# Gated mix of sliding-window attention and a GELU layer: one exponential tile per block of 128 keys, a masking step for both halves at once, wider steps of the division, and part-wise tiles in the last stage

## The chip, the cores and the metric

The kernel runs on one core of a Trainium2 chip. The metric is device time in microseconds (us), from the start to the end of one execution; the figure compared is the median of several executions.

## The reference

One input x of 2048 rows and 512 columns goes through two branches, and a gate per row mixes them:

```python
g = sigmoid((x * gate_w).sum(-1, keepdims=True))
a = attention(x)            # 32 heads of 16, window of 256 keys, causal; then @ wo
b = gelu(x @ w1 + b1) @ w2 + b2     # 512 -> 1792 -> 512
out = g * a + (1 - g) * b
```

In the attention, query i sees key j where 0 <= i - j < 256. The softmax is over these keys, and its result is multiplied with the values.

## The kernel before, in words

**Numbers.** All dense products (q, k, v, w1, w2, wo) are made in three matmuls each (`mm3`, L100): an operand is split into a rounded high part and the low remainder, and high*high, high*low and low*high are summed in PSUM. So each weight and each activation tile needs a copy on ScalarE (the high part) and a subtraction on VectorE or GpSimd (the low part).

**How the order is set.** The kernel is scheduled by hand: every engine runs its instructions in the order in which the program records them, and all DMAs stand in the one queue of SyncE (SP). While it records, the program keeps a clock of its own, `now`. `tick(ns)` moves it on with each group of matmuls, `after(ns, fn)` puts a step down for later, and `need(key)` runs such steps ahead until the one that makes `key` is recorded. The constants (`DIVS`, `HOLD`, `LAND0`, `LANDO`, `NORM`) are these delays: they say behind which other instructions a step stands, not when it runs. An instruction whose input isn't there holds up everything behind it on its engine.

**Stages.** `dense()` yields the dense matmuls in order: q, k and v of the four tiles of 512 rows (`qkv`, t = 0 to 3), the two layers of the GELU branch in eight turns (`mlp`, half of the 1792 features for one tile each), and the last product with wo (`final(t)`, t = 0 to 3). The attention runs between these matmuls (the loop at L859): for each of 8 groups of 4 heads and each of 16 blocks of 128 keys, one step `u` records four score matmuls for the row maxima (`att_max`, 12 blocks ahead), four for the exponentials (`att_exp`), and dense matmuls that fill the step.

**Maxima.** VectorE reduces the scores `sm` to maxima (`jm`, `M`, L472); `att_rows` turns them round (`nm`, `tt`), and GpSimd copies them as extra rows into `qs` (L495), so that the next score matmul `st` subtracts them.

**Exponentials.** `att_exp` (L501) works on a block of 128 keys in two halves `hf` of 64 keys, and in two pairs `pr`. ScalarE writes exp(st) into a tile `pt` (L531), one tile per half, 14 buffers. When both pairs of a half are written, `sel` clears the corners outside the window: four `affine_select` on GpSimd (L525; two partition halves, two edges) of 64 partitions by 2 x 64 numbers, or, in the last 12 blocks, one minimum on VectorE with a mask of 0 and 3e38 (L520).

**Values.** After every fourth block, `att_pvs` multiplies 6 blocks of `pt` with the values in `vbuf` (L553) and sums numerators and the denominator in two PSUM tiles, `pv_st` and `pv_sm`. The first pair of matmuls reads the first block and the second half of the last block. `vbuf` has two slots; `att_load_v` loads one (L453). ScalarE and VectorE add the two PSUM tiles into `nd` (L574, L577), which goes to DRAM (`ND`).

**Division.** For a pair of groups, `att_norm(t, c)` loads the denominators `den` from DRAM, takes the reciprocal (L595), stores them as `RD` (L598), loads the numerators `num` and the reciprocals spread over 16 rows `rb` (L603), multiplies them on VectorE (L607) and stores the result as `OT` (L610). `DIVS` holds the delays of these five steps.

**Last stage.** `load_o(t)` loads the four parts of `OT` of a tile (`ot`, L640) and splits them (L643, L646). `final(t)` makes 4 blocks of 12 matmuls each into PSUM tiles of which there are two; ScalarE scales the GELU branch (`ao`, L790), VectorE adds g times the PSUM tile (L817), and the sum is stored (L822). The GELU results come back through `load_y` (`qd<-YB`, `kd<-YB`, L784).

**Start.** In the first tile, `gate(0)` multiplies rows of x with the gate weights `gwb` on VectorE (`xj`, L269), and `load_xr(1)` loads the rows of the next tile into the buffers that this frees.

Of the kernel before, what the change touches and what calls it, by code (L numbers as in the profile page):

```python
# [32 lines left out]
def gated_mix(ctx: ExitStack, tc: tile.TileContext, x, wqkv, wo, w1, b1, w2, b2, gate_w, out):  # L33
# [94 lines left out]

    wk4 = wqkv.rearrange("(c p) f -> p c f", p=128)
    wt, raws = {}, {}  # L130

    def load_raw(key, early=False):
# [10 lines left out]
        elif early or now[0] < RAWS:  # L143
            raw = sb.tile([128, 2, 320], F32, tag="pt", bufs=PTS, name=f"raw_{kind}{i}")
            raw = raw.rearrange("p a b -> p (a b)")[:, 0:T]
        else:
            raw = sb.tile([128, T], F32, tag="raw", bufs=2, name=f"raw_{kind}{i}")
# [185 lines left out]
    def qkv(t):  # L333
# [17 lines left out]
        for n, (kind, j) in enumerate(pieces):  # L351
# [150 lines left out]
    def att_exp(g_, kb, i):  # L502
# [4 lines left out]
        if pr == 0:  # L507
            pts[g_, kb, hf] = sb.tile([128, 2, 320], F32, tag="pt", bufs=PTS, name=f"pt{g_}_{kb}_{hf}")
        pt = pts[g_, kb, hf]
# [5 lines left out]

        def sel():
            n = 1 + (w == W + 64)
            if g_ * NKB + kb >= NU - LEAD:
                v = pt.rearrange("p a (e x) -> p a e x", x=64)[:, :, 0:4 * n - 3:4]
                nc.vector.tensor_tensor(v, v, cut[:, 0:n].unsqueeze(1).broadcast_to([128, 2, n, 64]), op=ALU.min)  # L520
            else:
                for r in (0, 64):
                    for e in range(n):
                        v = pt[r:r + 64, :, W * e:W * e + 64]
                        nc.gpsimd.affine_select(out=v, in_=v, pattern=[[0, 2], [1 - 2 * e, 64]],  # L525
                                                compare_op=ALU.is_ge, fill=0.0, base=-e,
                                                channel_multiplier=2 * e - 1)
            done.add(("pt", g_, kb, hf))

        def exp():  # L530
            nc.scalar.activation(pt[:, pr, :w], p[:, :w], AF.Exp, scale=SCALE)  # L531
            if pr == 1:
                after(500, sel)
# [3 lines left out]
    def att_pvs(u):  # L537
# [21 lines left out]
        for j, pair in enumerate(pairs):  # L559
# [3 lines left out]
            for i in range(4):  # L563
                for hf, b in enumerate(pair):
                    k0 = b * 128 + hf * 64
                    q, e = max(k0, c * T), min(k0 + W + 64, S, (c + 1) * T)
                    mm(b, i, hf, q, e, lambda r: pts[g_, b, hf][r:r + 64, i // 2, q - k0:e - k0],
# [61 lines left out]
    def load_o(t, cs=range(NC)):  # L629

        if ("o", t) not in xts:
            if t % 2 == 0:
                v = sb.tile([128, NC, 2, T], F32R, tag="xt", bufs=1, name=f"ot{t}")
                xts["o", t] = [v[:, c] for c in range(NC)]
            else:
                xts["o", t] = [sb.tile([128, 2, T], F32R, tag="h", bufs=7, name=f"ot{t}_{c}") for c in range(NC)]
        ot = xts["o", t]
        for c in cs:
            need(("o", t, c))
# [306 lines left out]
```

## Time and profile before

| | us |
|---|---|
| median of 3 runs | 779.35 (777.29 to 779.69) |
| the profiled execution | 778.52 |
| its span in the profile | 776.8 |
| TensorE (PE) busy | 744.8 (96%) |
| VectorE (DVE) busy | 515.9 (66%) |
| ScalarE (ACT) busy | 431.6 (56%) |
| GpSimd (POOL) busy | 424.6 (55%) |

The span is what the profile's rows add up to; 1.7 us of the execution lie around it. A row of the timeline gives start, duration, engine, line, operation, output and inputs with shapes, and in brackets how long the engine had been idle and what ended that. SPq is the queue of SyncE, in which a row is the issue of a DMA and not its transfer; in the chain of waits, a row "DMA x<-y" is the time from issue to landing. PEclk is the clock granted to TensorE as a part of full speed. Matmuls overlap: the next one starts some 0.23 us after a 512-column one, though each is shown as 0.39 us long, and a busy PE may still not run at its peak.

### The profile page before, as it was taken

Reading aid. Unit: us, or ns where it says so; the run is one execution under the profiler, and the core shown is the slowest. Engines: PE = TensorE matmul, PEld = TensorE weight load, DVE = VectorE, ACT = ScalarE, POOL = GpSimd, SP = SyncE. Lnnn points to the kernel's source line nnn. Section 1 sums busy time; section 2 is a strip of 40 time slices with the busy share of each in tenths; the row PEclk is TensorE's granted clock in tenths of the full one; section 3 lists DMA queues with packets and bytes.
Section 4 is the critical chain, followed back from the end, with each engine's and each line's share of the span. In section 5 each row is a group of like instructions: output and inputs, shape, how many; then the busy total and the mean of one; then the engine's idle time right before and its main releaser. Section 6 shows DMA issues by size and latency. Waiting matters only on the chain.

```text
span 776.8 us, 18309 instructions
## 1 busy us (share of the span) xinstructions
PE 744.8 (96%) x6104; PEld 615.8 (79%) x6104; DVE 515.9 (66%) x1572; ACT 431.6 (56%) x973; POOL 424.6 (55%) x1174
## 2 busy tenths in 40 slices
PE   8999999989999999999999998999999999998798
PEld 6888888768788888888887877888888888876677
DVE  3532325789658877976896789568768866963443
ACT  4434523359448745854884587358647844974431
POOL 3200000239867976996797679669867976800000
PEclk9999999999999999999999999999999999999999
DMA  9979899998895798799676899986999998437672
GB/s 272 357 234 401 262 375 279 238 309 193 242 258 120 169 253 204 169 218 257 153 169 166 214 235 226 259 178 134 205 222 245 206 262 198 113 101 222 203 237 106
DMA packets 179262, 172.14 MB, mean 222 GB/s; under 512 B 56672, under 2 KB 122976, under 8 KB 179168
## 3 DMA queue, kind: packets, MB, share of 16 engines
q1 hardware_dynamic: 179168, 170.97, 83.4%
q8 instruction: 48, 0.79, 0.5%
q14 instruction: 46, 0.38, 0.2%
HBM read 108.53 MB, written 62.39 MB: 220 GB/s over the span
## 4 chain that ended last, share of the span: by engine, by line
PE 65%; DMA 13%; POOL 6%; DVE 6%; issue 3%; SPq 3%; ACT 3%; DVEq 0%; ACTq 0%; POOLq 0%
PE sm L467 7%; PE st L513 6%; PE pv_sm L553 6%; POOL pt L525 5%; DMA rb<-RD 5%; PE y L101 5%; PE u L101 4%; PE y L103 4%; PE y L102 4%; PE u L103 4%; PE u L102 4%; PE qk L101 4%; PE qk L103 3%; PE qk L102 3%; PE v L101 2%
## 5 line engine op out<-in xcount | busy, mean ns | idle before, releaser
L525 POOL TENSOR_SCALAR_AFFINE_SELECT pt<-pt 64x128 f32<-64x128 f32 x872 | 294.1, 357 | 102.7 <-ACT pt L531 82.0
L472 DVE CUSTOM_DVE_ANT_0 jm<-sm,mask 128x320 bf16<-128x320 f32 (+4 forms) x512 | 238.0, 465 | 74.4 <-PE sm L467 46.6
L531 ACT ACTIVATE pt<-st 128x320 f32<-128x320 f32 (+4 forms) x512 | 206.5, 423 | 132.3 <-PE st L513 128.5
L467 PE MATMUL sm<-kd,qd 96*128 96x320 f32 (+4 forms) x512 | 157.7, 311 | 5.2 <-DVE M L472 3.7
L513 PE MATMUL st<-qs,ks 128*128 128x320 f32 (+4 forms) x512 | 155.1, 307 | 2.4 <-ACT pt L531 2.4
L495 POOL CAST qs<-tt 4x256 fp32r<-4x256 f32 x256 | 116.9, 457 | 39.1 <-DVE tt L488 15.6
L467 PEld LDWEIGHTS sm<-kd,qd 96*128 96x128 f32 x512 | 96.5, 188 | 30.5 <-DVE M L472 9.1
L513 PEld LDWEIGHTS st<-qs,ks 128*128 128x128 f32 x512 | 98.0, 191 | 22.9 <-ACT pt L531 3.9
L101 PE MATMUL y<-w,h 128*128 128x512 f32 x224 | 90.7, 405 | 0.0
L103 PE MATMUL y<-w,h 128*128 128x512 f32 x224 | 88.6, 395 | 0.0
L553 PE MATMUL pv_st<-pt,vbuf 64*32 64x320 f32 (+4 forms) x1408 | 76.8, 355 | 12.2 <-POOL pt L525 4.4
L102 PE MATMUL y<-w,h 128*128 128x512 f32 x224 | 87.7, 392 | 0.0
L553 PE MATMUL pv_sm<-pt,vbuf 64*32 64x320 f32 (+4 forms) x1408 | 78.7, 355 | 2.4 <-DVE M L472 1.2
L101 PE MATMUL u<-mx,w 128*128 128x512 f32 x196 | 80.2, 409 | 0.0
L103 PE MATMUL u<-mx,w 128*128 128x512 f32 x196 | 77.5, 395 | 0.0
L102 PE MATMUL u<-mx,w 128*128 128x512 f32 x196 | 76.8, 392 | 0.0
L553 PEld LDWEIGHTS pv_sm<-pt,vbuf 64*32 64x32 f32 x1408 | 56.3, 108 | 19.9 <-DVE M L472 3.1
L553 PEld LDWEIGHTS pv_st<-pt,vbuf 64*32 64x32 f32 x1408 | 50.5, 108 | 13.4 <-POOL pt L525 7.3
L288 DVE TENSOR_TENSOR qke<-qk,qke 128x512 fp32r<-128x512 f32 x32 | 22.1, 690 | 48.1 <-ACT qke L285 40.0
L307 POOL MEMSET vx<- 128x32 f32 x16 | 2.5, 155 | 93.0 <-DMA kd<-SK 23.8
L574 ACT ACTIVATE nd<-pv_st 128x512 f32<-128x512 f32 x32 | 19.1, 597 | 57.5 <-PE pv_sm L553 53.4
L103 PEld LDWEIGHTS y<-w,h 128*128 128x128 f32 x224 | 42.1, 188 | 10.0
(142 smaller groups left out, 1336.3 us busy)
## 6 DMA issues: line engine op xcount, KB each, us to landing
kd<-SK SPq DMA_DIRECT2D x32, 384.0 KB
qs<-SQ SPq DMA_DIRECT2D x64, 192.0 KB
mx<-XT SPq DMA_DIRECT2D x24, 512.0 KB
SQ<-qke SPq DMA_DIRECT2D x16, 512.0 KB
SK<-qke SPq DMA_DIRECT2D x16, 512.0 KB
ND<-nd SPq DMA_DIRECT2D x32, 256.0 KB
raw_w<-in_B_w_dram SPq DMA_DIRECT2D x28, 256.0 KB
ks<-SK SPq DMA_DIRECT2D x32, 192.0 KB
```

The lines of the kernel that those rows point to most:

```text
L101: nc.tensor.matmul(p, lh, rh, start=first, stop=False)
L102: nc.tensor.matmul(p, lh, rl, start=False, stop=False)
L103: nc.tensor.matmul(p, ll, rh, start=False, stop=last)
L288: nc.vector.tensor_sub(e[:, 1 - h], p, f32(e[:, h]))
L467: nc.tensor.matmul(p[:, :w], qd[0:96, n, pr, 128 * j:128 * (j + 1)], kd[0:96, n, pr, k1 - w:k1], start=True, stop=True)
L472: nc.vector.tensor_tensor_reduce(junk[:, :w], p[:, :w], mask[:, 320 - w:320], 1.0, -3e38, ALU.add, ALU.max, M[:, 2 * (b % RB) + hb, pr:pr ...
L495: nc.gpsimd.tensor_copy(dst, src.unsqueeze(1).broadcast_to([4, 2, RB, 32]))
L513: nc.tensor.matmul(p[:, :w], ks[:, slot(g_, kb // NB), pr, at:at + 128], qs[:, pr, k0:k0 + w], start=True, stop=True)
L525: nc.gpsimd.affine_select(out=v, in_=v, pattern=[[0, 2], [1 - 2 * e, 64]], compare_op=ALU.is_ge, fill=0.0, base=-e, channel_multiplier=2 * ...
L531: nc.scalar.activation(pt[:, pr, :w], p[:, :w], AF.Exp, scale=SCALE)
L553: nc.tensor.matmul(pv[r // 64][32 * i:32 * i + 32, q - c * T:e - c * T], vts[g_, b // NB][r:r + 64, v:v + 32], rhs(r), start=start, stop=s ...
L574: nc.scalar.activation(nd, pv[0], AF.Copy)
```

## The change

Six things change. (1) A tile `pt` now holds a whole block of 128 keys (both halves), with 7 buffers for 14, and raw weights and output rows take half of such a tile each (`half_pt`). (2) Where GpSimd masks, it does so for both halves in one set of four `affine_select` of 64 x 4 x 64, behind the fourth exponential; the last of every four blocks keeps a set for each half. (3) The gate of the first tile and the load behind it are put 4 us later. (4) `vbuf` is asked for one step earlier. (5) In the division, the multiplication and the store stand further behind the loads; the last group pair uses the short delays for all four tiles, and its four sums are stored at once. (6) In the last stage each part of `ot` is a tile of its own, in buffers of the weights (t = 2) or of `h` (t = 1, 3), asked for only when its `OT` is stored, and tile t + 2 is asked for in the middle of `final(t)`.

```diff
+    spare = []
+    def half_pt(name):
+        if not spare:
+            v = sb.tile([128, 2, 2, 320], F32, tag="pt", bufs=PTS, name=name)
+            v = v.rearrange("p h a b -> p h (a b)")
+            spare.extend(v[:, h, 0:T] for h in (1, 0))
+        return spare.pop()
...
                 if n == 1:
-                    gate(0)
-                    load_xr(1)
+                    after(4000, gate, 0)
+                    after(4000, load_xr, 1)
...
+        n = 1 + (w == W + 64)
+        late = g_ * NKB + kb >= NU - LEAD
+        both = not late and kb % NB < NB - 1
         def sel():
...
+                hs = slice(0, 2) if both else slice(hf, hf + 1)
                 for r in (0, 64):
                     for e in range(n):
-                        v = pt[r:r + 64, :, W * e:W * e + 64]
-                        nc.gpsimd.affine_select(out=v, in_=v, pattern=[[0, 2], [1 - 2 * e, 64]],
+                        v = pt[r:r + 64, hs].rearrange("p h a c -> p (h a) c")[:, :, W * e:W * e + 64]
+                        nc.gpsimd.affine_select(out=v, in_=v, pattern=[[0, v.shape[1]], [1 - 2 * e, 64]],
...
-            if pr == 1:
+            if pr == 1 and (hf == 1 or not both):
                 after(500, sel)
...
-            after(HOLD if g_ * NT + c < NQ - 2 else 800, store)
+            after(HOLD if g_ * NT + c < NQ - 4 else 800, store)
...
-                after(NORM if g_ * NT + c < NQ - 2 else 3500, att_norm, c, g_ // 2)
+                after(NORM if g_ * NT + c < NQ - 4 else 3500, att_norm, c, g_ // 2)
...
-            done.add(("o", t, c))
-        for ns, fn in zip(DIVS[c == NC - 1 and t >= NT - 2], (rcp, keep, back, mul, store)):
+            after(REACH, done.add, ("o", t, c))
+        for ns, fn in zip(DIVS[c == NC - 1], (rcp, keep, back, mul, store)):
...
+    def load_part(t, c, land, skew):
+        ot = xts["o", t]
+        if ("o", t, c) not in done:
+            return after(500, load_part, t, c, LANDO, 0)
+        if t:
+            tag, bufs = ("w", 14) if t == 2 else ("h", 7)
+            ot[c] = sb.tile([128, 2, T], F32R, tag=tag, bufs=bufs, name=f"ot{t}_{c}")
+        nc.sync.dma_start(f32(ot[c][:, 1]), OT[t][c])
...
     def final(t):
+        if t == 0:
+            load_o(1)
...
-            if t == NT - 2 and b == 2:
-                load_o(t + 1, range(NC - 1, NC))
+            if b == 2 and t < 2:
+                load_o(t + 2, range(NC - t))
+            if b == 1 and t == 2:
+                load_o(NT - 1, range(NC - 1, NC))
...
-        if u % NB == 1 and u >= 0:
+        if u % NB == 0 and u >= 0:
             att_load_v(*divmod(u // NB, NT))
...
-PTS = 14
+PTS = 7
+REACH = 2500.0
-DIVS = ((6000, 9000, 12000, 18500, 22000), (4500, 5700, 8500, 13500, 15000))
+DIVS = ((6000, 9000, 12000, 21500, 23500), (4500, 5700, 8500, 17000, 18500))
```

The order of the matmuls on PE stays as it was. Three places on other engines follow. First SyncE's queue early in the attention, at the second load of `vbuf` (SV1 are the values of the second tile; SK2 keys, XT3 the kept x, ND0_0 the first sums). Before:

```order
L425 DMA ks_181<-SK2_76 48x2x64
L730 DMA XT3_85<-xt3_984 128x1024 x4
L622 DMA mx00_2152<-XT0_82 128x1024
L447 DMA qs_180<-SQ3_73 48x2x512 x2
L453 DMA vbuf_175<-SV1_79 128x8x34
L581 DMA ND0_0_90<-nd0_0_2114 128x512
```

After:

```order
L435 DMA ks_181<-SK2_76 48x2x64
L463 DMA vbuf_175<-SV1_79 128x8x34
L750 DMA XT3_85<-xt3_980 128x1024 x4
L636 DMA mx00_2123<-XT0_82 128x1024
L457 DMA qs_180<-SQ3_73 48x2x512 x2
L595 DMA ND0_0_90<-nd0_0_2084 128x512
```

The load of `vbuf` now stands ahead of the four XT stores, the mx load and both qs loads.

Second, VectorE near the end, at the first division of the last group pair (pt7_10 and pt7_11 are blocks 10 and 11 of the last group, num0_3 the product for tile 0, yo the GELU result). Before:

```order
L520 TENSOR_TENSOR pt7_10_1_10715<-pt7_10_1_10715,cut_151 128x2x2x64
L520 TENSOR_TENSOR pt7_11_0_10731<-pt7_11_0_10731,cut_151 128x2x2x64
L748 SCALAR_TENSOR_TENSOR yo_10722<-y3_11_10679,ya3_11_10092 128x512
L607 TENSOR_TENSOR num0_3_10738<-num0_3_10738,rb0_3_10740 128x512
L595 RECIPROCAL den1_3_10752<-den1_3_10752 128x32
L520 TENSOR_TENSOR pt7_11_1_10749<-pt7_11_1_10749,cut_151 128x2x2x64
```

After:

```order
L533 TENSOR_TENSOR pt7_10_10243<-pt7_10_10243,cut_151 128x2x2x64
L621 TENSOR_TENSOR num0_3_10193<-num0_3_10193,rb0_3_10195 128x512
L533 TENSOR_TENSOR pt7_11_10271<-pt7_11_10271,cut_151 128x2x2x64
L768 SCALAR_TENSOR_TENSOR yo_10262<-y3_11_10222,ya3_11_9644 128x512
L609 RECIPROCAL den1_3_10248<-den1_3_10248 128x32
L533 TENSOR_TENSOR pt7_11_10271<-pt7_11_10271,cut_151 128x2x2x64
```

The product num0_3 stands two instructions further ahead; the reciprocal of den1_3 keeps its place in front of the second mask of block 11.

Third, SyncE's queue at the same time (ks are keys of the last tile, qd<-YB0 and YB1 GELU results). Before:

```order
L591 DMA den0_3_10570<-ND0_3_93 128x1x32
L428 DMA ks_181<-SK3_77 48x8x128
L423 DMA ks_181<-SK3_77 48x7x128
L425 DMA ks_181<-SK3_77 48x2x64
L581 DMA ND1_3_97<-nd7_1_10651 128x512
L598 DMA RD0_3_109<-den0_3_10570 128x32
L453 DMA vbuf_175<-SV2_80 128x8x34
L784 DMA qd_182<-YB0_126 128x2x512 x2
L603 DMA num0_3_10738<-ND0_3_93 128x1x512
L603 DMA rb0_3_10740<-RD0_3_109 128x1x512
```

After:

```order
L605 DMA den0_3_10052<-ND0_3_93 128x1x32
L612 DMA RD0_3_109<-den0_3_10052 128x32
L617 DMA num0_3_10193<-ND0_3_93 128x1x512
L617 DMA rb0_3_10195<-RD0_3_109 128x1x512
L595 DMA ND1_3_97<-nd7_1_10189 128x512
L438 DMA ks_181<-SK3_77 48x8x128
L433 DMA ks_181<-SK3_77 48x7x128
L435 DMA ks_181<-SK3_77 48x2x64
L463 DMA vbuf_175<-SV2_80 128x8x34
L804 DMA qd_182<-YB0_126 128x2x512 x2
```

The loads num0_3 and rb0_3 now stand ahead of the keys, of vbuf and of YB0. For the next tile it is the other way round: the store of RD1_3, which stood ahead of the two loads of YB1, now stands behind them.

More of the change, by code (lines that the diff above doesn't have):

```diff
@@ L143, in load_raw @@
         elif early or now[0] < RAWS:
-            raw = sb.tile([128, 2, 320], F32, tag="pt", bufs=PTS, name=f"raw_{kind}{i}")
-            raw = raw.rearrange("p a b -> p (a b)")[:, 0:T]
+            raw = half_pt(f"raw_{kind}{i}")
         else:
+            spare.clear()
             raw = sb.tile([128, T], F32, tag="raw", bufs=2, name=f"raw_{kind}{i}")
@@ L635, in load_o, with hi, lo @@
             else:
-                xts["o", t] = [sb.tile([128, 2, T], F32R, tag="h", bufs=7, name=f"ot{t}_{c}") for c in range(NC)]
+                xts["o", t] = {}
+        for n, c in enumerate(cs):
+            load_part(t, c, LAND0 if t == 0 else LANDO, 700 * n)
+    def load_part(t, c, land, skew):
         ot = xts["o", t]
-        for c in cs:
-            need(("o", t, c))
-            nc.sync.dma_start(f32(ot[c][:, 1]), OT[t][c])
-            def hi(c=c):
-                nc.scalar.activation(ot[c][:, 0], f32(ot[c][:, 1]), AF.Copy)
-            def lo(c=c):
-                nc.vector.tensor_sub(ot[c][:, 1], f32(ot[c][:, 1]), f32(ot[c][:, 0]))
-                done.add(("ot", t, c))
-            n = cs.index(c)
-            land = LAND0 if t == 0 else LANDO
-            after(land + 700 * n, hi), after(land + 700 * n + 600, lo)
+        if ("o", t, c) not in done:
[4 more added lines that the diff above has]
+        nc.sync.dma_start(f32(ot[c][:, 1]), OT[t][c])
+        def hi():
+            nc.scalar.activation(ot[c][:, 0], f32(ot[c][:, 1]), AF.Copy)
+        def lo():
+            nc.vector.tensor_sub(ot[c][:, 1], f32(ot[c][:, 1]), f32(ot[c][:, 0]))
+            done.add(("ot", t, c))
+        after(land + skew, hi), after(land + skew + 600, lo)
     TURNS = [(0, 3), (0, 0), (0, 1), (0, 2), (1, 2), (1, 0), (1, 1), (1, 3)]
@@ L793, in final @@
     def final(t):
+        if t == 0:
+            load_o(1)
         ot = xts["o", t]
-        if t < NT - 1:
-            load_o(t + 1, range(NC) if t < NT - 2 else range(NC - 1))
         for b in range(NB):
```

21 lines of the change are left out of this document (9 added, 12 removed).

## The prediction

> **What bounds the kernel now.** I read the page first: TensorE is busy nearly all the time.
>
> ```profile
> span 776.8 us, 18309 instructions
> PE 744.8 (96%) x6104; PEld 615.8 (79%) x6104; DVE 515.9 (66%) x1572; ACT 431.6 (56%) x973; POOL 424.6 (55%) x1174
> ```
>
> So 32.0 us of the span have no matmul, and the change leaves the matmuls as they are: its gain lies in those 32.0 us and in a slower clock, nowhere else. Next the view of busy time by stage. Its columns are the stretch, its length, then PE, PEld, DVE, ACT and POOL busy, the granted clock, DMA share and GB/s.
>
> ```profile
> 250.00:450.00 200.00, 196.11 (x1931) 164.20 (x1929) 154.62 (x510) 124.23 (x282) 159.71 (x446) 1.00 0.84 197
> 700.00:720.00 20.00, 16.28 (x156) 12.86 (x154) 6.25 (x14) 8.31 (x23) 0.00 (x0) 0.91 0.82 229
> 720.00:740.00 20.00, 15.59 (x147) 12.57 (x148) 9.77 (x19) 7.69 (x13) 0.00 (x0) 0.94 0.52 180
> ```
>
> In the attention PE idles 2%; from 700 to 740 us it idles 3.7 + 4.4 = 8.1 us of 40, and the clock falls to 0.91 and 0.94 there. The last stage is where most is lost. Then the timeline of PE, for the idle time before a matmul and what ended it:
>
> ```profile
> 18.66 0.50 PE L101 MATMUL qk<-ks,qk 128*128 128x512 f32 x1 [0.96 <-DVE qke L288]
> 205.69 0.25 PE L553 MATMUL pv_st<-pt,vbuf 64*32 64x64 f32 x2 [1.94 <-DMA vbuf<-SV]
> 341.31 0.30 PE L553 MATMUL pv_sm<-pt,vbuf 64*32 64x64 f32 x2 [1.03 <-DVE M L472]
> 483.69 0.30 PE L553 MATMUL pv_st<-pt,vbuf 64*32 64x64 f32 x4 [1.69 <-POOL pt L525]
> 706.17 0.25 PE L553 MATMUL pv_st<-pt,vbuf 64*32 64x64 f32 x2 [3.55 <-issue]
> 722.15 0.25 PE L553 MATMUL pv_st<-pt,vbuf 64*32 64x64 f32 x2 [2.32 <-DVE pt L520]
> 737.90 0.76 PE L101 MATMUL a<-wo,ot 128*128 128x512 f32 x1 [2.26 <-DVE ao L817]
> 751.42 0.47 PE L101 MATMUL a<-wo,ot 128*128 128x512 f32 x1 [0.83 <-DVE ao L817]
> ```
>
> The row at 483.69 stands for nine like it, which the view of waits sums (us in total, times, longest):
>
> ```profile
> PE pv_st L553 <- POOL pt L525: 4.4, 5, 1.7
> PE pv_sm L553 <- POOL pt L525: 1.1, 4, 0.3
> ```
>
> Five causes: 0.96 us at the start, 1.94 for vbuf, 5.5 for GpSimd's masks, 1.03 at 341 us and 3.55 + 2.32 + 2.26 + 0.83 = 8.96 near the end, 18.4 of the 32.0 us. The timeline of VectorE says what is behind three of them.
>
> ```profile
> 16.96 1.03 DVE L269 CUSTOM_DVE_ANT_0 xj<-xr,gwb 128x512 bf16<-128x512 f32 x1 [3.47 <-DMA gwb<-in_gate_w_dram]
> 340.06 0.79 DVE L607 TENSOR_TENSOR num<-num,rb 128x512 f32<-128x512 f32 x1 [1.33 <-DMA rb<-RD]
> 704.84 0.69 DVE L607 TENSOR_TENSOR num<-num,rb 128x512 f32<-128x512 f32 x1 [4.41 <-DMA rb<-RD]
> 705.71 0.69 DVE L520 TENSOR_TENSOR pt<-pt,cut 128x256 f32<-128x256 f32 x2
> ...
> 749.32 0.69 DVE L607 TENSOR_TENSOR num<-num,rb 128x512 f32<-128x512 f32 x1 [2.71 <-DMA rb<-RD]
> ```
>
> And the view of waits has all of this kind:
>
> ```profile
> DVE num L607 <- DMA rb<-RD: 20.1, 8, 5.0
> ```
>
> VectorE stands at the product num and waits for rb, four of the eight times from 704 to 750 us. Behind it in its order stand the masks of the last blocks (705.71) and the evictions of the last stage, and PE waits for those: each of the four late stalls of PE starts in a wait of num. The "issue" at 706.17 is this too, since the masks are done at 706.4.
>
> **The change part by part.** *Gate of the first tile.* The gate product waits 3.47 us for gwb, and the eviction qke behind it comes late. 4 us later in the order, qke of two more matmul groups stands ahead, and gwb has landed. The loads of xr move behind one store of keys and the first of XT; their first transpose comes over 7 us later, which hides them. Gain 0.9, between 0 and the 0.96 of the row.
>
> *vbuf.* From the queue of SyncE and the chain of waits:
>
> ```profile
> 187.87 3.66 SPq L730 DMA_DIRECT2D XT<-xt  x4
> 199.86 0.54 SPq L453 DMA_DIRECT2D vbuf<-SV  x1
> 199.86 5.69 DMA vbuf<-SV
> ```
>
> vbuf now stands ahead of XT, so is issued at about 188 and lands at 188 + 5.7 = 194, 11 us ahead of need. Its slot is free, as it is the first use. Later vbuf loads wait for the value matmuls just recorded, and the store of nd waits behind them; none was late before. Gain 1.9 (0 to 1.94).
>
> *Masks.* The groups of GpSimd, shapes apart (count, busy us, mean ns):
>
> ```profile
> L525 POOL TENSOR_SCALAR_AFFINE_SELECT pt<-pt 64x128 f32<-64x128 f32 x872 | 294.1, 357 | 102.7 <-ACT pt L531 82.0
> L80 POOL TENSOR_SCALAR_AFFINE_SELECT cut<-cut 64x64 f32<-64x64 f32 x4 | 0.9, 236 | 0.1
> masks.py:199 POOL TENSOR_SCALAR_AFFINE_SELECT ident<-ident 128x128 f32<-128x128 f32 x1 | 0.3, 292 | 0.1
> ```
>
> Seven groups have 14 blocks of 8 selects and 2 of 4, the eighth 4 blocks of 8: 7 x 120 + 32 = 872. Three blocks of every four now take half as many, of 256 numbers: 11 blocks of 4 and one of 2 a group, 3 of 4 in the eighth, 7 x 46 + 12 = 334. The fourth blocks keep 7 x 28 + 8 = 204 of 128. No row has 256 numbers. From 64 to 128 a select grows by 292 - 236 = 56 ns undisturbed (0.88 ns a number) or 357 - 236 = 121 ns as it runs in the attention (1.9 ns). So 128 more cost 113 to 242 ns: 470 to 599 ns; the upper bound is twice 357, with nothing saved. I take 470, as the attention's 357 holds waiting beside the work. GpSimd then saves 668 x 0.357 - 334 x 0.47 = 238.5 - 157.0 = 81.5 us of its 424.6 (38.4 at 599).
>
> By the Trainium skill's "GPSIMD Engine Reference", section 3.1, an element costs about 2.6 cycles in a two-input add; at that and its 1.2 GHz, 128 more would be an estimated 277 ns, a select 634, and the saving 27 us. By that rule a third of the stall would go (1.8 us), and the sum would be 2.7 us smaller; the 0.88 ns between the two set-up rows speak against it.
>
> PE waits because GpSimd is behind, not because one mask is slow: ahead of 483.69 it ran 28 selects back to back.
>
> ```profile
> 475.24 10.77 POOL L525 TENSOR_SCALAR_AFFINE_SELECT pt<-pt 64x128 f32<-64x128 f32 x28
> ```
>
> The last block of every four, for which PE waits, keeps its two short sets; ahead of it stand three blocks at half the count, some 12 x (2 x 0.357 - 0.47) = 2.9 us less backlog, against stalls of 1.69 us at most. That later masks of the first half wait for the fourth exponential costs nothing: the values need them blocks later. Gain 4.5, between 1.8 and 5.5.
>
> *Division in the attention.* num stands some three maxima later in the order.
>
> ```profile
> L472 DVE CUSTOM_DVE_ANT_0 jm<-sm,mask 128x320 bf16<-128x320 f32 x448 | 217.7, 486 | 69.1 <-PE sm L467 44.4 <-PE st L513 3.6 <-DVE M L472 0.5
> ```
>
> rb landed 1.33 us late, three maxima take 1.46, so the 1.03 us at 341 go; the other such waits cost PE little. Gain 1.0 (0 to 1.03).
>
> *Last group.* The chain of waits shows how long the DMAs of a division take:
>
> ```profile
> 432.42 6.01 DMA RD<-den
> 577.65 3.30 DMA RD<-den
> 581.00 4.65 DMA rb<-RD
> 695.78 8.96 DMA rb<-RD
> 705.55 3.04 DMA OT<-num
> ```
>
> For tile 0 rb was issued at 695.78, behind two loads of YB0, and took 8.96 us. VectorE before that:
>
> ```profile
> 686.32 0.69 DVE L670 SCALAR_TENSOR_TENSOR x1h<-sqh,x1h 128x512 f32<-128x512 f32 x1 [1.27 <-ACT sqh L667]
> ...
> 697.72 0.43 DVE L520 TENSOR_TENSOR pt<-pt,cut 128x256 f32<-128x256 f32 x1 [0.47 <-ACT pt L531]
> ```
>
> The reciprocal now stands just ahead of the first of these two rows, so RD goes out by about 687; rb follows 3.3 to 6.0 us later, ahead of YB0, and lands 4.7 to 9.0 us after: between 695 and 702. num, behind the mask of the last row, is reached at about 698. The stall of 3.55 us then shrinks to between 0 and 3. For tile 1, RD1_3 now stands behind YB1, and SyncE waits for its landing before rb; but everything starts 3.5 us earlier, and num stands three masks later. For tiles 2 and 3 num stands behind one more eviction or more, and rb is issued a few us earlier against its eviction. Each of the four can be cured or be half left: gain 6.5 of 8.96, between 2 and 8.96. Who is late next: the masks themselves, 0.3 to 0.4 us each.
>
> *Clock.* At 0.91 and 0.94, 16.28 and 15.59 us of matmuls lose 1.5 + 0.9 = 2.4 us; the dips stand beside the idle time. If most of that goes, about half: 1.2 (0 to 2.4).
>
> *Tiles of the last stage.* t = 2 no longer waits for the one xt tile. No matmul waited long for that, so 0; it costs where loads come later, which is the second rival.
>
> *Given back.* PE comes earlier to the maxima of a busy VectorE:
>
> ```profile
> PEld sm L467 <- DVE M L472: 9.1, 17, 1.3
> ```
>
> Mean 0.54 us; I count four more such waits, 2.0 us (0 to 4).
>
> **Sum**: 0.9 + 1.9 + 4.5 + 1.0 + 6.5 + 1.2 - 2.0 = 14.0 us. The profiled execution took 778.52, 1.7 over its span and 0.8 under the median of 779.35. 778.5 - 14.0 = 764.5, and 765 as a median. All best ends: 778.5 - 20.8 = 758 (the 18.4 us of stalls and 2.4 of clock); all worst: 1.8 + 2 - 4, or 779.
>
> **The rivals.** *The last stage keeps its stalls.* DMAs there are slow because the queues are full (share 0.82 from 700 to 720 us), not because of their order: rb stays late, num blocks again, RD1_3 behind YB1 does it. Then the tail and clock terms go: 0.9 + 1.9 + 4.5 + 1.0 - 2.0 = 6.3, giving 772 to 773. For it speaks that 1 MB of YB is loaded either way, against it that rb of tile 0 overtakes it. Chance 0.17.
>
> *Slower: the last stage's loads come late.* Each ot is asked for only after its OT is recorded as stored, and stands behind output stores which wait for evictions. The split of a part that has landed is two passes over 128x512; at the 0.69 of VectorE's rows an estimated 1.4 us. From RD to the split it is 3.30 + 4.65 + 3.04 + 1.4 = 12.4 us at best, by the rows above, and 6.01 + 8.96 + 3.04 + 1.4 = 19.4 at worst; a tile of `final` gives 48 matmuls at
>
> ```profile
> 751.89 0.23 PE a L102
> ```
>
> 11.0 us. Where the chain of a tile starts only as the tile before it starts, 1.4 to 8.4 us are uncovered. It decides from 6.3 us on, which is what the other parts bring. At 6 us for two tiles: 778.5 - 6.3 + 12 = 784. Against it: in the order the OT store of tile 2 stands in front of tile 1's first output, and tile 3's in front of tile 1's last, a whole tile ahead. Chance 0.08.
>
> *Nothing moves.* The masks grow to 714 ns and PE, freed at one engine, waits for the next (VectorE is busy 154.62 of 200 us in the attention); the tail's gain and new waits cancel. 778 to 779. Chance 0.06.
>
> **How the numbers follow.** The forecast has 0.69, and 765. A measurement of this kernel tells about 0.3% (2.3 us) from no change. Faster by more: 0.69 + 0.17 = 0.86; within: 0.06; slower: 0.08. The range goes from 757.5, the best end, to 775, which takes in the first rival and leaves out the two others and some 0.04 of the rest.
>
> **What would show it.** GpSimd: 538 selects, 334 of them of 256 numbers near 470 ns, and no row of PE waiting for POOL over 0.5 us. vbuf issued ahead of XT, no PE wait for it. No wait of qke at 18 us. VectorE's wait for rb down from 20.1 us to under 6, PE idle from 700 to 740 us down from 8.1 to under 4, clock there over 0.95. Wrong: selects at 600 or more, a num that still waits 3 us with a mask behind it, or matmuls of `final` waiting for ot.

## The result, and the profile after

| | before | after |
|---|---|---|
| median of 4 runs | 779.52 (777.29 to 780.33) | 757.25 (755.88 to 758.3) |
| the profiled execution | 778.52 | 756.76 |
| its span | 776.8 | 755.0 |
| mean clock granted to TensorE | 0.991 | 0.998 |

The ratio is 0.9718, with a 95% interval of 0.9692 to 0.9744: some 22 us, where 14 were forecast. The page after:

```profile
span 755.0 us, 17908 instructions
PE 737.6 (98%) x6104; PEld 607.0 (80%) x6104; DVE 521.1 (69%) x1572; ACT 431.5 (57%) x973; POOL 364.6 (48%) x840
```

PE is idle for 17.4 us of the span where it was for 32.0, and busy for 7.2 us less with the same matmuls. So two thirds of the gain are idle time, and the rest is that the same matmuls took less time: 5.1 us of it by the clock (below), the other 2.1 us weren't taken apart. The view by stretch, for the same stretches as before:

```profile
250.00:450.00 200.00, 198.06 (x1939) 164.65 (x1938) 158.76 (x515) 127.06 (x288) 137.66 (x314) 1.00 0.87 203
700.00:720.00 20.00, 18.67 (x171) 15.24 (x170) 11.73 (x22) 10.04 (x23) 0.00 (x0) 1.00 0.71 221
720.00:740.00 20.00, 20.00 (x90) 16.57 (x89) 10.30 (x16) 9.93 (x17) 0.00 (x0) 1.00 0.77 257
```

From 700 to 740 us 1.3 us are idle for 8.1, at full clock. What PE still waits for there is one wait, in the view of waits; the row for masks has sunk from 5.5 us to 0.3, and what was given back stands in the two rows of sm:

```profile
PE sm L477 <- DVE M L482: 4.3, 6, 1.2
PE sm L477 <- DVE nd L591: 2.2, 3, 0.8
PE pv_st L567 <- DVE pt L533: 1.3, 1, 1.3
PE pv_sm L567 <- POOL pt L539: 0.3, 1, 0.3
```

GpSimd's groups after (count, busy us, mean ns), the copies of the extra rows last, and that last row before:

```profile
L539 POOL TENSOR_SCALAR_AFFINE_SELECT pt<-pt 64x256 f32<-64x256 f32 x334 | 153.1, 479 | 95.2 <-ACT pt L545 89.6
L539 POOL TENSOR_SCALAR_AFFINE_SELECT pt<-pt 64x128 f32<-64x128 f32 x204 | 71.5, 369 | 26.2 <-ACT pt L545 21.2
L505 POOL CAST qs<-tt 4x256 fp32r<-4x256 f32 x256 | 126.9, 496 | 70.8 <-DVE tt L498 24.2 <-PE sm L477 23.6 <-PE st L523 12.2
```

```profile
L495 POOL CAST qs<-tt 4x256 fp32r<-4x256 f32 x256 | 116.9, 457 | 39.1 <-DVE tt L488 15.6 <-PE sm L467 11.2
```

The masks cost 224.6 us for 294.1; 10.0 us come back in the copies, which take 39 ns longer each.

Since the matmuls stand in the same order in both kernels, the two traces can be laid over each other: for each pair of neighbouring matmuls, the time from start to start before, less that after. Summed over stretches of the trace before:

| stretch, us | gained, us | where |
|---|---|---|
| 0 to 25 | 1.2 | the first eviction (1.1) |
| 150 to 200 | -0.5 | maxima |
| 200 to 250 | 2.2 | vbuf (2.15), a mask (0.8), less 0.6 |
| 325 to 350 | 1.4 | num at 341 us (1.1) |
| 400 to 450 | 1.9 | masks (1.6) |
| 475 to 500 | 3.9 | masks (2.4), and matmuls that run at full clock |
| 550 to 650 | 0.5 | masks (2.1), less maxima (1.8) |
| 700 to the end | 11.6 | the four late stalls (8.2), and matmuls at full clock |
| elsewhere | -0.4 | |
| all | 21.8 | the difference of the spans |

**The clock.** In the trace before, up to the last matmul, its dips are all alike: 3.4 us long, at half clock, and their starts lie whole multiples of 3.413 us apart (174.55, 485.16, 707.03 and 737.75: 91, 65 and 9 of them). The view by stretch of the trace before, cut at these multiples (length, PE busy, then at the third place from the end the clock):

```profile
481.75:485.16 3.41, 1.44 (x49) 1.04 (x56) 2.66 (x8) 0.44 (x1) 3.17 (x10) 1.00 1.03 259
485.16:488.57 3.41, 3.41 (x63) 2.45 (x43) 0.00 (x0) 0.54 (x1) 3.05 (x10) 0.50 1.17 200
720.68:724.09 3.41, 1.94 (x79) 1.72 (x87) 1.42 (x6) 0.32 (x1) 0.00 (x0) 1.00 0.56 198
724.09:727.50 3.41, 3.41 (x40) 2.72 (x22) 1.58 (x3) 1.82 (x3) 0.00 (x0) 1.00 0.39 103
734.34:737.75 3.41, 1.31 (x6) 0.75 (x4) 2.56 (x5) 0.22 (x1) 0.00 (x0) 1.00 0.40 149
737.75:741.16 3.41, 3.26 (x8) 2.61 (x9) 2.04 (x5) 0.00 (x0) 0.00 (x0) 0.50 0.24 56
```

Where PE was idle for 1.97 or 2.10 us of such a window, the next one ran at 0.50; behind 1.47 us it did not, though the stall at 722.15 (2.32 us) is longer than that at 737.90 (2.26): it lies across a boundary. Each window at half clock costs 3.41 / 2 = 1.7 us. Before had four of them, after has one, at 172 us, where it had one before too: 5.1 us.

### The profile page after: what moved, and what is told of

It is laid out like the page before. It is cut to its first block, busy times and chain, and to the rows that moved or that the text cites. A ratio compares the mean times of both kernels' runs of the same rounds, so it can differ in the third digit from the quotient of the medians.

```text
span 755.0 us, 17908 instructions
## 1 busy us (share of the span) xinstructions
PE 737.6 (98%) x6104; PEld 607.0 (80%) x6104; DVE 521.1 (69%) x1572; ACT 431.5 (57%) x973; POOL 364.6 (48%) x840
## 4 chain that ended last, share of the span: by engine, by line
PE 87%; DVE 4%; DMA 4%; issue 2%; ACT 2%; SPq 0%; POOL 0%; DVEq 0%; ACTq 0%
PE sm L477 9%; PE st L523 9%; PE pv_sm L567 7%; PE y L101 7%; PE y L103 6%; PE y L102 6%; PE u L101 6%; PE u L103 6%; PE u L102 6%; PE qk L103 4%; PE qk L101 4%; PE qk L102 4%; PE pv_st L567 2%; PE v L103 2%; PE v L102 2%
## 5 line engine op out<-in xcount | busy, mean ns | idle before, releaser
L539 POOL TENSOR_SCALAR_AFFINE_SELECT pt<-pt 64x256 f32<-64x256 f32 (+1 forms) x538 | 224.6, 438 | 121.4 <-ACT pt L545 110.8
L505 POOL CAST qs<-tt 4x256 fp32r<-4x256 f32 x256 | 126.9, 496 | 70.8 <-DVE tt L498 24.2
L567 PE MATMUL pv_sm<-pt,vbuf 64*32 64x320 f32 (+4 forms) x1408 | 74.0, 346 | 0.5 <-POOL pt L539 0.3
L567 PE MATMUL pv_st<-pt,vbuf 64*32 64x320 f32 (+4 forms) x1408 | 73.0, 346 | 1.3 <-DVE pt L533 1.3
L567 PEld LDWEIGHTS pv_sm<-pt,vbuf 64*32 64x32 f32 x1408 | 51.2, 106 | 19.3 <-DVE M L482 1.9
L295 ACT ACTIVATE qke<-qk 128x512 fp32r<-128x512 f32 x32 | 19.1, 597 | 50.2 <-PE qk L103 28.9
L567 PEld LDWEIGHTS pv_st<-pt,vbuf 64*32 64x32 f32 x1408 | 46.1, 106 | 1.6 <-DVE pt L533 1.5
```

What stands on the lines that cost most here:

```text
L295: nc.scalar.activation(e[:, h], p, AF.Copy)
L505: nc.gpsimd.tensor_copy(dst, src.unsqueeze(1).broadcast_to([4, 2, RB, 32]))
L539: nc.gpsimd.affine_select(out=v, in_=v, pattern=[[0, v.shape[1]], [1 - 2 * e, 64]], compare_op=ALU.is_ge, fill=0.0, base=-e, channel_multi ...
L567: nc.tensor.matmul(pv[r // 64][32 * i:32 * i + 32, q - c * T:e - c * T], vts[g_, b // NB][r:r + 64, v:v + 32], rhs(r), start=start, stop=s ...
```

## The experiments

Each ratio is against the kernel before on the same chip, with its interval; the changed kernel has 0.9718. At 778 us, 0.01 is 7.8 us. Single times of one kernel scatter by up to 10 us, one reason being a stall of 1.6 to 2.7 us near 620 us, put down to "issue", that five of the traces below show (kernels 3, 6, 7, 8 and 9) and the others don't. So the place in the trace decides beside the time.

**1. Sets apart.**

```diff
-        both = not late and kb % NB < NB - 1
+        both = False
```

> The changed kernel, but GpSimd masks each half by itself again in every block (872 selects of 128 numbers). Theory (GpSimd's backlog): the changed trace has 0.35 us of PE waiting for masks where the trace before had 5.5, and one window of half clock less (1.7 us) behind the wait at 483.69. Both come back, less 1 to 2 us that later waits of PE for maxima give back: 762 to 765 us, PE waits for POOL over 4 us in the span. Rival (the whole-block tile with its 7 buffers is what helps, or the waits just move): 756 to 759 us, PE waits for POOL under 1.5 us.

Measured: 765.09 us, 0.9838 (0.9804 to 0.9872), 9 us over the changed kernel; span 763.9. The waits of PE for masks:

```profile
PE pv_st L567 <- POOL pt L539: 5.1, 5, 1.5
PE pv_sm L567 <- POOL pt L539: 1.9, 6, 0.6
```

7.0 us are back, and a window at half clock at 482.6 us. The time is 0.1 us above the theory's range. The rival falls: with the tile of a whole block kept, the gain goes when the sets are apart. What that tile does by itself, without joined sets, was not tried.

**2. Joined masks alone**, on the kernel before: the tiles of a whole block and these lines of the change, and no other of its parts.

```diff
+        both = not late and kb % NB < NB - 1
...
-            if pr == 1:
+            if pr == 1 and (hf == 1 or not both):
                 after(500, sel)
```

> The kernel before with the whole-block tiles and the joined masks alone (the division's delays, the loads of the last stage, vbuf and the gate as before). Undone in the changed kernel, the joined masks were worth 8.9 us of the span, 1.7 of them a window of half clock. Theory (GpSimd's backlog is a limit of its own, the gain adds to the others): 7.5 to 9.5 us faster than before, 768 to 770 us. Rival (TensorE, freed of GpSimd, comes earlier to products num that wait for rb with maxima behind them, and gives a third or more back there): 771 to 774 us, with over 2 us more of waits for M and nd than before.

Measured: 771.23 us, 0.989 (0.9862 to 0.9918): 8 us faster than before, with a span of 768.7 for 776.8. The difference is what the theory said (the median of before was 779.34 there, so 771 is 8 less). PE's waits for M and nd at sm didn't grow (4.8 us for 5.1). So the masks' share of 8 to 9 us adds to the others.

**3. Start as before**: the gate and its load at once, and vbuf a step later.

```diff
-                    after(4000, gate, 0)
-                    after(4000, load_xr, 1)
+                    gate(0)
+                    load_xr(1)
...
-        if u % NB == 0 and u >= 0:
+        if u % NB == 1 and u >= 0:
```

> The changed kernel with the gate of the first tile and the load behind it at once, and vbuf one step later, both as before. Theory: 0.96 to 1.1 us at 18 us and 1.9 to 2.2 us at the first vbuf come back, with no window of half clock: 759.5 to 761 us. Rival (each of these stalls is only moved to the next wait of PE): 757 to 758 us, PE idle in all within 0.7 us of the changed kernel's 17.4.

Measured: 759.62 us, 0.9766 (0.9733 to 0.9799). The stall of 0.96 us at 18 us is back word for word. Of vbuf's 1.94 us only 0.22 came back at its old place, and waits of up to 1.0 us at two other loads of it (1.7 us in all). How late vbuf comes differs, then, from one execution and one load to another: the four traces in which it stands at the old place show PE waiting for that load for 0.22 to 2.00 us (kernels 2, 3 and 6, and the kernel before), and none of the ten with the new place has such a wait there. Laid over the changed kernel's, the matmuls lost 1.1 at the gate and 0.4, 0.7 and 1.2 us at vbuf: the theory's sum, at other places than it said.

The time doesn't decide between theory and rival. The interval overlaps the changed kernel's, and 4.7 of the 4.9 us by which this execution is longer are the stall near 620 us and its window. Against the losses stand gains of 0.6 to 1.0 us each at 163, 218, 581 and 599 us, which make up for most of them, as the rival would have it. Gains of 0.4 to 1.0 us at these places show in other kernels' traces too, which leave the start alone, so they may be scatter. What the start is worth in time stays open.

**4. Division as before.**

```diff
-            after(HOLD if g_ * NT + c < NQ - 4 else 800, store)
+            after(HOLD if g_ * NT + c < NQ - 2 else 800, store)
...
-                after(NORM if g_ * NT + c < NQ - 4 else 3500, att_norm, c, g_ // 2)
+                after(NORM if g_ * NT + c < NQ - 2 else 3500, att_norm, c, g_ // 2)
...
-        for ns, fn in zip(DIVS[c == NC - 1], (rcp, keep, back, mul, store)):
+        for ns, fn in zip(DIVS[c == NC - 1 and t >= NT - 2], (rcp, keep, back, mul, store)):
...
-DIVS = ((6000, 9000, 12000, 21500, 23500), (4500, 5700, 8500, 17000, 18500))
+DIVS = ((6000, 9000, 12000, 18500, 22000), (4500, 5700, 8500, 13500, 15000))
```

> The changed kernel with the old delays of the division: the old DIVS, and HOLD, NORM and the short row for the last two tiles only. Theory (the place of num and rb in the order ends the late stalls): the stalls behind num near the end come back, 6 to 8 us of idle PE from 690 us on and up to two windows of half clock (3.4 us), and 1 us in the attention: 764 to 769 us. Rival (the loads of the last stage in parts, or the earlier start of the whole stage, ended them): 757 to 760 us, under 3 us of idle PE from 690 us on besides the 1.33 that the changed kernel has.

Measured: 766.01 us, 0.985 (0.9811 to 0.9889), 10 us over the changed kernel. VectorE's waits are back, 18.6 us of them; its four products near the end:

```profile
697.16 0.69 DVE L621 TENSOR_TENSOR num<-num,rb 128x512 f32<-128x512 f32 x1 [1.69 <-DMA rb<-RD]
712.94 0.68 DVE L621 TENSOR_TENSOR num<-num,rb 128x512 f32<-128x512 f32 x1
720.98 0.69 DVE L621 TENSOR_TENSOR num<-num,rb 128x512 f32<-128x512 f32 x1 [3.38 <-DMA rb<-RD]
734.88 0.69 DVE L621 TENSOR_TENSOR num<-num,rb 128x512 f32<-128x512 f32 x1 [4.94 <-DMA rb<-RD]
```

The theory holds with a remarkable gap: num of tiles 0, 2 and 3 waits again, and that of tile 1, which had waited 4.99 us, does not. TensorE stalls behind tile 2 for 2.4 us in two pieces and behind tile 3 for 2.9, with a window at half clock; behind tile 0, whose num waits 1.69 us (4.41 before), it doesn't stall. Something else in the change has cured tile 1, so the place of num and rb isn't the whole cause.

**5. Loads of the last stage as before**: `load_o`, its calls and the tiles it uses are taken from the kernel before; the division keeps its new delays.

```diff
-            after(REACH, done.add, ("o", t, c))
+            done.add(("o", t, c))
...
+        for c in cs:
+            need(("o", t, c))
+            nc.sync.dma_start(f32(ot[c][:, 1]), OT[t][c])
```

> The changed kernel with the loads of the last stage as before: one tile for t = 0 and 2 in turn, whole tiles asked for at the start of the stage's turn before. Theory (no matmul waits for these loads, the late stalls are num's alone): 756 to 759 us. Rival (the parts asked for apart carry a share of the 11.6 us that the matmuls from 700 us on gained): 761 us or more, with PE waiting for ot, or VectorE for rb, from 700 us on.

Measured: 766.82 us, 0.9861 (0.9825 to 0.9898). The theory falls, and with it a line of the prediction. The profiled execution is one of the shorter ones (763.67), and its span is 7.0 us over the changed kernel's. In the timeline of PE one stall is left near the end, and VectorE's num of tile 1 is behind it:

```profile
709.43 0.32 PE L567 MATMUL pv_st<-pt,vbuf 64*32 64x64 f32 x2 [4.89 <-DVE pt L533]
```

```profile
706.28 0.69 DVE L621 TENSOR_TENSOR num<-num,rb 128x512 f32<-128x512 f32 x1 [5.28 <-DMA rb<-RD]
```

Two windows at half clock follow (707.9 to 714.8 us). SyncE's queue in this trace, and below it in the changed kernel's (rows between them left out):

```profile
688.99 0.32 SPq L624 DMA_DIRECT2D OT<-num  x1
693.69 0.32 SPq L654 DMA_DIRECT2D ot<-OT  x1
...
694.57 0.39 SPq L612 DMA_DIRECT2D RD<-den  x1
695.01 2.14 SPq L798 DMA_DIRECT2D qd<-YB  x2
...
698.85 0.59 SPq L617 DMA_DIRECT2D rb<-RD  x1
```

```profile
688.61 0.32 SPq L624 DMA_DIRECT2D OT<-num  x1
...
689.45 1.29 SPq L804 DMA_DIRECT2D qd<-YB  x2
690.84 0.71 SPq L612 DMA_DIRECT2D RD<-den  x1
693.85 0.33 SPq L662 DMA_DIRECT2D ot<-OT  x1
...
697.35 0.59 SPq L617 DMA_DIRECT2D rb<-RD  x1
```

The old load of ot stands right behind the store of OT that it reads, and SyncE waits 4.7 us until that has landed. In the changed kernel two things are issued in that time: YB1, two loads of 512 KB, and RD. That left two causes: RD is held, or YB1 passes right in front of rb. The next four kernels ask which.

**6. New delays of the division alone**, on the kernel before.

> The kernel before with the new delays of the division alone (DIVS, and the short row, HOLD 800 and NORM 3500 for all four tiles of the last pair). The run with the loads in parts undone gave back 7.0 us of the span near the end, the one with the old division 7.8 of 11.6: either alone would then bring 4 to 5. Theory (two causes of rb's lateness that share the late stalls: num's place, and SyncE's queue held by a load of ot that waits for its OT): 4 to 7 us faster than before, with a wait of num for rb of over 3 us left near 705 us and SyncE idle in front of RD. Rival (the division's delays bring the whole gain, and the parts only repair what the new delays would spoil): 10 us or more faster, waits of num for rb under 3 us in all. Other rival (the delays alone move RD of the next tile behind YB1 and bring nothing): within 2 us of before.

Measured: 772.18 us, 0.992 (0.9896 to 0.9944), 6 us faster than before: the theory's size. Both signs of the theory are there: num of tile 1 waits 4.99 us for rb, and SyncE waits 4.7 us (698.76 to 703.45) ahead of RD. Of the four late stalls one of over 1 us is left, that of tile 1, and it grew from 2.32 to 4.61 us, though num waits 4.99 us before and here. 1.0 us of the growth is that two splits of ot now stand between num and the last mask (3.10 us from num's start to that mask's end, for 2.09); the rest wasn't taken apart. Tile 3 is not quite cured: num waits 2.31 us there (2.71 before), TensorE 0.56 (0.83 before).

**7. The load of ot ahead of RD.**

```diff
-REACH = 2500.0
+REACH = 0.0
```

> The changed kernel with REACH at 0. In SyncE's order this exchanges two rows near the end: the load of the fourth part of ot for tile 0, which waits for its OT store to land, then stands ahead of the store RD of tile 1 and not behind it. Theory (that load holds SyncE's queue for some 4 us, and RD with it): RD of tile 1 goes out at 693 to 695 us, not at 690.8, num then waits 3 to 5 us for rb near 705 us, and the time is 3 to 9 us longer: 760 to 766 us. Rival (it is the tiles apart, that is the buffers, that ended the stalls): 756 to 759 us, no wait of num over 1 us.

Measured: 759.37 us, 0.9759 (0.9714 to 0.9805); the interval overlaps the changed kernel's. The edit moves a little more than the expectation says: the loads of the fourth part of ot for tiles 2 and 3 move as well, and the splits behind them. RD went out at 697.30, 5.8 us behind the OT store of tile 0 (691.52) for 2.2, as the theory had it; but num waited 0.98 us, not 3 to 5:

```profile
706.51 0.69 DVE L621 TENSOR_TENSOR num<-num,rb 128x512 f32<-128x512 f32 x1 [0.98 <-DMA rb<-RD]
```

TensorE lost 1.3 us from 700 us on, 0.9 of them at 739 us, where the last parts of ot come later. From the chain of waits:

```profile
691.52 5.33 DMA OT<-num
697.30 4.71 DMA RD<-den
702.02 4.46 DMA rb<-RD
```

RD is held, and that costs little here, as rb took only 4.46 us. In kernel 5, in the same view:

```profile
688.99 4.68 DMA OT<-num
694.57 4.26 DMA RD<-den
698.85 7.41 DMA rb<-RD
```

Counted from the issue of OT, rb landed after 15.0 us here and after 17.3 in kernel 5. What differs on the way is YB1: issued 9.3 us ahead of rb here, 3.8 us ahead in kernel 5. That is 2.3 of the 4.3 us between the two waits. The other 2.0 are num's place: in kernel 5 one split of ot and one mask fewer stand ahead of it on VectorE, which reaches it 12.0 us behind the issue of OT, and after 14.0 here. The held queue had fallen as the main cause, and the next kernel moves YB1 alone.

**8. YB1 right ahead of rb.**

```diff
-            load_y((u % NKB - 9) // 2)
+            after(3000 if u % NKB == 11 else 0, load_y, (u % NKB - 9) // 2)
```

> The changed kernel with the two loads of YB1 3 us later: in SyncE's order they move from ahead of RD and of the held load of ot to right ahead of num and rb of tile 1. Nothing else moves. Where rb was issued 2 to 4 us behind two loads of YB it has taken 7.0 to 9.0 us (four times in three runs), and 4.5 us where it was issued 9 us behind them. Theory (what the parts asked for apart brought is that YB1's 1 MB passes while the OT store lands, and not in front of rb): rb takes 7 to 9 us, num waits 2 to 5 us for it near 705 us, TensorE stalls behind it, and the time is 759.5 to 766 us. Rival (the held queue is the cause, and here RD goes out as early as in the changed kernel): 756 to 758.5 us, num waits under 1 us.

Measured: 763.6 us, 0.9816 (0.978 to 0.9851), 8 us over the changed kernel. RD goes out 2.95 us behind the OT store (694.90, 691.95), rb 3.0 us behind YB1:

```profile
691.95 5.09 DMA OT<-num
700.45 8.59 DMA rb<-RD
```

```profile
709.06 0.69 DVE L621 TENSOR_TENSOR num<-num,rb 128x512 f32<-128x512 f32 x1 [3.56 <-DMA rb<-RD]
```

From 700 us on TensorE loses 4.2 us: 2.6 of stall and a window at half clock. The theory holds, the rival falls: with every other instruction in its place, YB1 right ahead of rb brings back 3.56 of the 5.28 us that num waits in kernel 5. The rest is nearly all num's place, 1.5 us as counted above. (3.9 us more of the time are the stall near 620 us and its window.)

**9. YB1 behind rb**, with 5000 for 3000 in the same line.

> The changed kernel with the two loads of YB1 5 us later: in SyncE's order they then stand behind num and rb of tile 1, next to those of YB2. Theory (only what stands close ahead of rb counts): rb of tile 1 takes under 5 us, num does not wait near 705 us, 755 to 758.5 us; the gain is spent already. Rival (2 MB in a row now stand in front of the sums and RD of tile 2): num of tile 2 waits 2 us or more, 759 us or more.

Measured: 761.12 us, 0.978 (0.9735 to 0.9824). num waits nowhere near the end, so the rival's wait doesn't come, and tile 1 is cured here too; but the theory's time is missed. The stretch from 700 us on is 1.3 us longer, not shorter. PE waits there for the last load of vbuf, which was issued at 703.75, 2.0 us behind YB1, and landed 8.1 us later; in the changed kernel, where YB1 stands 9.1 us ahead of it, PE doesn't wait for it:

```profile
711.90 0.25 PE L567 MATMUL pv_st<-pt,vbuf 64*32 64x64 f32 x2 [1.88 <-DMA vbuf<-SV]
```

So, by this one trace, the same 1 MB delays another short load instead. The time itself settles nothing, since 3.7 of the other microseconds are the stall near 620 us and its window, and 2.8 lie at 215 us.

**10. Held evictions.**

```diff
-            nc.vector.tensor_sub(e[:, 1 - h], p, f32(e[:, h]))
+            for _ in range(1 + HELD.get((t, j), 0)):
+                nc.vector.tensor_sub(e[:, 1 - h], p, f32(e[:, h]))
...
+HELD = {(1, 0): 4, (1, 5): 5, (1, 3): 6, (2, 0): 7, (2, 5): 5, (2, 3): 6}
```

> The changed kernel with six evictions of q and k (tiles 1 and 2) repeated 4 to 7 more times on VectorE, 0.6 us each, so that TensorE idles about 1.3, 1.9, 2.5, 3.1, 1.9 and 2.5 us at places some 8 us and more apart, where it is else always busy. Theory (the clock is granted by windows of 3.41 us that run on by themselves: where TensorE idled over about half of one, the next runs at half clock and costs 1.7 us): every window with over 1.84 us of idle time is followed by one of half clock, none with under 1.52 is; 2 to 5 such windows, 773 to 780 us in all. Rival (only a gap near a whole window long drops the clock): at most one, behind the gap of 3.1 us, 770 to 773 us. Other rival (each single gap of over 1.7 us drops it, wherever it falls): five.

Measured: 776.28 us, in one execution. The six gaps were 1.51, 1.90, 2.64, 3.68, 1.90 and 2.64 us. Two gaps of the same length, in the timeline of PE:

```profile
76.78 0.50 PE L101 MATMUL v<-v,qd 128*128 128x512 f32 x1 [2.64 <-DVE qke L299]
...
122.62 0.72 PE L101 MATMUL v<-v,qs 128*128 128x512 f32 x1 [2.64 <-DVE qke L299]
```

The view by stretch, cut at the multiples of 3.413 us of this execution:

```profile
74.96:78.37 3.41, 1.59 (x7) 1.34 (x8) 2.89 (x5) 1.08 (x2) 0.00 (x0) 1.00 0.28 105
78.37:81.78 3.41, 3.41 (x19) 2.79 (x18) 0.56 (x1) 1.28 (x5) 0.00 (x0) 1.00 1.03 381
...
119.33:122.74 3.41, 0.77 (x4) 0.30 (x3) 3.27 (x6) 0.60 (x1) 0.00 (x0) 1.00 0.39 145
122.74:126.15 3.41, 3.41 (x9) 2.67 (x10) 1.02 (x2) 0.00 (x0) 0.00 (x0) 0.50 0.64 235
```

The first lay across a boundary, left 1.82 us idle in its fullest window and cost nothing more; the second lay in one window and was followed by one at half clock. The 3.68 us were followed by one too, the three gaps under 2 us by none. The theory holds, and both rivals fall. A third window at half clock came at 10 us, behind one with 1.58 us idle, so the bound isn't sharp.

**11. Weights split later**, to see whether the window at 172 us can go.

```diff
-LAND = 7500.0
+LAND = 11000.0
```

> The changed kernel with LAND at 11000 for 7500: the split of a weight is put down 3.5 us later behind its load. In the changed trace ScalarE and VectorE wait 4.0 and 1.9 us for a raw weight at 163 us, PE waits 1.23 us twice and 0.86 once for what stands behind, and a window of half clock follows (1.7 us). Theory: two of these waits and the window go: 752.5 to 755 us. Rival (the wait is moved to the matmul that needs the weight, or to the next maxima): 756.5 to 759 us, with a half-clock window left near 172 us.

Measured: 768.19 us, 0.9867 (0.9814 to 0.992). Both miss: the window near 172 us is gone, but one comes at 220 us, and a new wait of 9.9 us stands at 481 us, for a weight, with three windows at half clock.

```profile
480.89 0.79 PE L101 MATMUL y<-w,h 128*128 128x512 f32 x1 [9.91 <-ACT w L171]
```

By the code, these later weights share two buffers, which the change holds longer, so that the next load starts later; that was not tried by itself.

**12. The first 14 weights alone.**

```diff
-            after(LAND, split, key, nc.vector)
+            after(LAND + 3000, split, key, nc.vector)
```

> The changed kernel with the split of a weight 3 us later behind its load, for the first 14 weights of the GELU layer alone (those loaded before RAWS). With all weights later, the stalls at 162 to 172 us shrank by some 1.5 us only, and a new wait of 10 us came at 471 us. Theory (the late weights alone made that wait, and the early ones still bring what is there): 754 to 756.5 us, the 10 us gone. Rival (the waits for weights near 163 us hide behind VectorE's maxima anyway): 756.5 to 758.5 us with a half-clock window left near 172 us.

Measured: 756.49 us, 0.9722 (0.9688 to 0.9755): no change. The matmuls from 150 to 175 us gain 4.4 us, the window at 172 us among it, and from 175 to 200 us 2.9 us are lost again. The time lies where the two forecasts meet; that the gain is given back is the rival's, though its window is gone.

## Why the prediction was right or wrong

The sign was right, and each named stall went or shrank, all but that of tile 1 for the reason given; the size was 14 us for 22. The measured median lies 0.25 us under the range's best end: nearly everything that could go went at once. Step by step:

- **Gate** (0.9): 1.1, by the matmuls laid over each other, and back in kernel 3.
- **vbuf** (1.9): 2.15 between the two traces. It was issued at 186.62, ahead of XT as said. Kernel 3 brought back 1.7 at three places, so its size is that of one execution: 0.22 to 2.00 in four traces.
- **Masks** (4.5): the waits fell from 5.5 to 0.3 us, 5.2. The selects took 479 ns, where 470 to 599 was the range and 470 the choice. By the Trainium skill's "GPSIMD Engine Reference", section 3.1, the estimate was 634; no run shows that. Undone, the masks were worth 9 us (kernel 1), and alone on the kernel before 8 (kernel 2): the term had no window of half clock, and one stood behind 483.69.
- **Division in the attention** (1.0): 1.1 at 341 us.
- **Last group** (6.5): the four stalls of 8.96 us became one of 1.33, so 7.6. At that one num doesn't wait; it is the mask behind a split of ot, which the prediction had priced at 0.3 to 0.4. Tiles 2 and 3 need the division's delays (kernel 4 brings their stalls back), and tile 3 not them alone: kernel 6 keeps 0.56 of its 0.83 us. For tile 0 they are enough (kernel 6), but without them TensorE doesn't stall there either (kernel 4).
- **Tiles of the last stage** (0): this step failed. "No matmul waited long for that, so 0" looked at who waits for ot, and not at what stands behind ot in SyncE's queue. Tile 1 was cured there: with the old loads it alone stalls, for 4.9 us and two windows (kernel 5). The prediction had put its hope for tile 1 on the earlier start and on num's place three masks later. Kernel 5 keeps the delays that give both, and tile 1 stalls. The prediction had also counted "RD1_3 now stands behind YB1" as a risk. What counts is that YB1 then doesn't stand close ahead of rb (kernels 8 and 9). So tile 1's share of the term was right by luck.
- **Clock** (1.2): 5.1. This is the term that was mis-sized. It was an average over 40 us, halved; the windows at half clock cost 1.7 us each, and three of the four went with their stalls. Two of these three lay near 707 and 738 us, the third, at 485 us, was hidden in a stretch of 200 us at 0.99. By the Trainium skill's "TensorE: Matmul & The Clock Gate", Part 1, a window of 3413 ns that runs on by itself sets the clock, half after an idle one; its section "HAM oscillation" asks for no gap over some 3.4 us. The runs agree on the window's length, on its running on, and on half. They differ on how idle: over 1.85 us of 3.41 was enough.
- **Given back** (2.0): PE's waits for M and nd at sm rose from 5.1 to 6.5 us, 1.4.

Together 1.1 + 2.15 + 5.2 + 1.1 + 7.6 + 5.1 - 1.4 = 20.9 of the 21.8 us.

Of the rivals, "the last stage keeps its stalls" fell with its reason: order decides. It was right that YB1 slows what stands behind it: behind YB1, RD took 6.5 us at most (690.84 to the issue of rb at 697.35), and 4.3 us ahead of YB1 in kernel 5. But that is less than rb loses where YB1 stands close ahead of it. "The loads come late" did not occur: PE never waits for ot in the changed kernel. "Nothing moves" is excluded by the interval.

Left open: what the "issue" near 620 us waits for, and why some windows fall to half clock behind 1.58 to 1.84 us of idle time when others don't behind as much.

## What to carry to other kernels

A short load costs what the queue does ahead of it, as vbuf and rb show here: ask, of each large transfer that moves, which small one on the critical path now stands within some 4 us behind it, and of each load that waits for a store, what stands behind it in its queue. Price a stall of a busy TensorE of about 2 us or more with a window at half clock, which adds 1.7 us where the idle time falls into one window of 3.41 us and not across two, and look for these windows in stretches of 5 us, since long ones average them away. Two fixes of the same chain have to be undone one at a time: here each showed tiles that the other had not cured.

## What the runs showed of the hardware that was not expected

- In all traces with a dip, among whole windows between the first and the last matmul, the window of 3.413 us behind one in which TensorE had idled over 1.85 us ran at half clock. Below 1.58 us a full clock never fell. In between both occurred. A clock already at half stayed there with 1.49 us idle (kernel 5).
- rb, 256 KB, took 4.5 us where YB's 1 MB had been issued 9.3 us ahead of it (kernel 7), and 7.0 to 9.0 us where that was 1.7 to 3.9 us ahead (five times, in kernels 5, 6 and 8 and in the kernel before).
- With fewer and longer selects on GpSimd, its copies of 4x256 took 496 ns for 457, though nothing in them changed; with the sets apart they took 458.
